# The first weight load of a decode block in one transfer or in four strided ones

## The chip, the cores and the metric

The kernel runs on one core of a Trainium2 chip. Its time is the device time of one execution in microseconds, the median of several runs. Before the change it is 437.96 us (three runs, 437.83 to 437.99). A difference under 0.2% of this, 0.88 us, is not told from no change here.

## The reference

One decode step of a transformer block with eight sequences: a conditioning vector gives six modulation vectors, then come attention over a key and value cache (grouped heads) and a gated feed-forward part. Cut to what is computed:

```python
mod = silu(c) @ w_mod                     # (8,1024) @ (1024,6144) -> sa, ca, ga, sb, cb, gb
h = layernorm(x) * (1 + ca) + sa
q = h @ wq                                # (8,1024) @ (1024,4096): 32 heads of 128
o = softmax(q . k_cache / sqrt(128)) @ v_cache   # 8 sequences, 4 groups, 8192 keys of 128
x = x + ga * (o @ wo)                     # (8,4096) @ (4096,1024)
h = layernorm(x) * (1 + cb) + sb
x = x + gb * ((relu(h @ W_gate) * (h @ W_up)) @ W_down)
```

Weights and caches are bf16. Nearly all of the bytes are the two caches, 64 MB each; everything is read once.

## The kernel before

All large inputs go through one ring in the on-chip memory: 128 partitions by five slots A to E of 32 KB each (`ring`, line 278). A list `stream` (lines 345 to 384) names every load in order: `("wq", 0)`, `("wq", 1)`, `("mod", 0)`, `("mod", 1)`, then the blocks of the key cache `("k", n)` and the value cache `("v", n)` for 16 steps, with the two halves of `wo` between, then gate, up and down weights. A block of a cache, of `wq` or of `wo` is 4 MB: every partition gets one contiguous piece of 32 KB. A half of `w_mod` is 6 MB (48 KB for each partition).

`("wq", 0)` is the first load of all. `A_wq` is viewed as `(p k) n -> p k n` with eight rows for each partition, and the block takes the first four of them (line 352), so partition p reads 32 KB that lie at 64 KB times p in HBM, and writes them to slot D. Its semaphore is that of slot D, shared with the value blocks that come into the slot later (`"v1"`); the table `counts` (line 403) holds the value that the semaphore has when a load is complete, 16 for each transfer.

All these loads are issued by SyncE (SP in the profile), in the order of the list, at line 747. A load into a slot waits until the matmuls that read the slot's former block are done (`users`, `behind`; line 748); the first four loads wait for nothing. ScalarE issues two small loads, of `c` and `x` (8 rows of 2 KB each, lines 472 and 473), at the same time.

TensorE reads in another order than the loads come: first the small work on `c` and `x` (silu, transposes, layernorm), then the matmuls of the modulation with `("mod", 0)` and `("mod", 1)` (line 511), then the projection to q with `("wq", 0)` and `("wq", 1)` (line 529), then the loop over the cache blocks, the output projection, the feed-forward part and the stores. In the profile all matmuls through the helper `mm` have line 422, all transposes line 426, all VectorE work line 430, ScalarE work line 433.

The two lines that the load goes through:

```python
counts[sk] = counts.get(sk, 0) + 16                                                           # 403
o.fn = (lambda e, key=key, src=src, o=o: e.dma_start(place[key], src).then_inc(o.sem, 16))    # 747
```

Of the kernel before, what the change touches and what calls it, by code (L numbers as in the profile page):

```python
# [234 lines left out]
def bass_adaLN_cond__gqa_block_cached__glu_gated_reglu__decode_kernel(  # L235
# [33 lines left out]
    with ExitStack() as es:  # L269
# [77 lines left out]
        def block(key, at, cols, src, shape, slot=None):  # L347
            stream.append((key, at, cols, src, shape, slot))
# [34 lines left out]
        block(("wd", 3), B_ + 11 * D, 2 * D, wd[:, 3, 4:6], (2, D))  # L383
        block(("wd", 4), B_ + 13 * D, D, wd[:, 3, 6:7], (1, D))

        place = {}
        held = []
        behind = []
# [2 lines left out]
        counts = {}  # L391
        rsem = {}
        for key, at, cols, src, shape, slot in stream:
            lo, hi = at, at + cols
            behind.append([k for l, h, k in held if l < hi and h > lo])
            held = [x for x in held if not (x[0] < hi and x[1] > lo)] + [(lo, hi, key)]
            t = ring[:, lo:hi]
            place[key] = (t.rearrange("p (a n) -> p a n", n=shape[1]) if len(shape) == 2
                          else t.rearrange("p (a i n) -> p a i n", i=shape[1], n=shape[2]))
            sk = slot or key  # L400
            if sk not in rsem:
                rsem[sk] = E(nc.semaphore("d_r%d" % len(rsem)))
            counts[sk] = counts.get(sk, 0) + 16
            o = _Op("sp", None, 0)
            o.sem = rsem[sk]
            o.semval = counts[sk]
            loads[key] = o
# [319 lines left out]
        for c_ in (2, 3):  # L727
            for i in range(7):
                if c_ == 2:
                    key, w = ("wd", 1), place[("wd", 1)][:, i, :]  # L730
                else:
                    u = 2 + (i >= 4) + (i >= 6)
                    key, w = ("wd", u), place[("wd", u)][:, i - (0, 4, 6)[u - 2], :]
# [10 lines left out]
        head = []  # L744
        for i, (key, at, cols, src, shape, slot) in enumerate(stream):
            o = loads[key]
            o.fn = (lambda e, key=key, src=src, o=o: e.dma_start(place[key], src).then_inc(o.sem, 16))
            o.deps = [users[k] for k in behind[i]] + ([users["v", -1]] if key == ("v", 1) else [])
            head.append(o)
        g.prog["sp"] = head + g.prog["sp"]  # L750
# [33 lines left out]
```

## Time and profile before

| | before |
|---|---|
| median of 3 runs | 437.96 us |
| span of the profiled execution (first to last instruction) | 436.3 us |
| bytes read from HBM | 185.63 MB |
| TensorE / VectorE / ScalarE busy | 307.2 / 180.0 / 208.4 us |
| loads of `wq` | 2 of 4096 KB, issued at 0.7 and 1.2 us |
| matmuls of the q projection | 59.18 to 62.85 us |

The profile is of one execution; its span stands 1.66 us (437.96 less 436.3) under the median of the runs, and this lies around the span, before the first instruction and after the last. The profile divides time by engine: PE is TensorE's matmul, PEld its weight load, DVE is VectorE, ACT is ScalarE, SP is SyncE, with a "q" behind the name for the part that only issues. The DMA engines, 16 of them, carry all transfers; the profile gives their mean busy share and the bytes that they moved. A transfer consists of packets; in this kernel a packet is one contiguous piece for one partition. The chain of waits is the chain of work that ended last, followed back from the last instruction. In windows of the trace a packet is counted in the window in which it starts, so over a window shorter than a packet the share and the rate can exceed what the engines can do.

### The profile page before, as it was taken

To read this page: it belongs to the slowest core of one execution; us is meant where nothing else is said; L and a number is where in the kernel's file an instruction comes from. 1 tells how busy PE (TensorE), PEld (TensorE's weight loads), DVE (VectorE), ACT (ScalarE), POOL (GpSimd) and SP (SyncE) were. 2 spreads that over 40 slices of the span, in tenths; PEclk is the share of its full clock that TensorE was granted. 3 is DMA by queue.
4 is the path that set the end of the run, shared out by engine and by line. 5 is a ranking of instruction groups with operands and counts; after the bars stand their busy time and mean duration, and the time that the engine had idled before them with its cause. 6 is when DMAs were issued, how large, how long until landed. Compare 5 with 4: busy or idle time off the path is not lost.

```text
span 436.3 us, 10723 instructions
## 1 busy us (share of the span) xinstructions
PE 307.2 (70%) x4575; PEld 200.1 (46%) x4575; DVE 180.0 (41%) x384; ACT 208.4 (48%) x246; POOL 12.6 (3%) x52
## 2 busy tenths in 40 slices
PE   0104257989878888787888888777888878755356
PEld 0101025656555555554555555555555555432323
DVE  3600036456363644536264553536364453331111
ACT  2200005676756747675664757576575747400000
POOL 6000000000000000000000000000000000000000
PEclk9999599999999999999999999999999999885766
DMA  8999999999999999999999999999999999999996
GB/s 339 433 433 446 431 431 432 434 431 431 433 436 433 436 433 436 433 436 433 433 436 433 436 436 433 433 436 436 433 436 433 433 433 433 420 422 439 430 419 251
DMA packets 7003, 185.81 MB, mean 426 GB/s; under 512 B 800, under 2 KB 832, under 8 KB 1104
## 3 DMA queue, kind: packets, MB, share of 16 engines
q1 hardware_dynamic: 6928, 185.61, 98.8%
q8 instruction: 9, 0.15, 0.1%
q10 hardware_dynamic: 64, 0.04, 0.0%
q14 instruction: 2, 0.02, 0.0%
HBM read 185.63 MB, written 0.02 MB: 426 GB/s over the span
## 4 chain that ended last, share of the span: by engine, by line
DMA 54%; PE 23%; DVE 9%; issue 8%; ACT 5%; SPq 0%; DVEq 0%; ACTq 0%; POOL 0%
DMA ring<-in_A_k_cache_dram 34%; PE PS L422 13%; DMA ring<-in_w_mod_dram 11%; PE PS L426 11%; DMA ring<-in_B_W_down_dram 8%; ACT P L433 3%; DVE KT L430 2%; ACT KT L433 2%; DVE tm L430 2%; DVE ov L430 1%; DVE nm L430 1%; DVE mp L430 1%; DVE rl L430 0%; DVE nb L430 0%; DVE qT L430 0%
## 5 line engine op out<-in xcount | busy, mean ns | idle before, releaser
L433 ACT ACTIVATE KT<-PS 128x1024 bf16<-128x1024 bf16 (+1 forms) x130 | 131.9, 1016 | 164.2 <-PE PS L426 137.7
L426 PE MATMUL PS<-identb,ring 128*128 128x128 bf16 x2048 | 152.8, 220 | 22.0 <-DMA ring<-in_A_k_cache_dram 20.3
L430 DVE COPY KT<-PS 128x1024 bf16<-128x1024 bf16 (+1 forms) x129 | 88.9, 689 | 164.2 <-PE PS L426 129.1
L426 PEld LDWEIGHTS PS<-identb,ring 128*128 128x128 bf16 x2048 | 117.0, 98 | 61.3 <-issue 36.9
L422 PE MATMUL PS<-KT,Z 128*32 128x512 bf16 x516 | 51.9, 389 | 0.1
L422 PE MATMUL PS<-ring,pt 128*32 128x256 bf16 x1088 | 49.8, 274 | 0.6 <-DVE pt L430 0.6
L433 ACT ACTIVATE P<-PS,nb 64x1024 bf16<-64x1024 f32 x34 | 37.7, 1108 | 6.2 <-DVE nb L430 4.2
L426 PE MATMUL PS<-identb,P 128*128 128x128 bf16 x272 | 21.1, 221 | 20.2 <-ACT P L433 14.5
L422 PEld LDWEIGHTS PS<-ring,pt 128*32 128x32 bf16 x1088 | 24.5, 95 | 12.8 <-issue 0.8
L422 PE MATMUL PS<-ring,siluT 128*24 128x512 bf16 x96 | 8.6, 531 | 27.6 <-DMA ring<-in_w_mod_dram 27.6
L426 PEld LDWEIGHTS PS<-identb,P 128*128 128x128 bf16 x272 | 15.5, 98 | 26.5 <-DVE KT L430 17.2
L433 ACT ACTIVATE pt<-PS 64x512 bf16<-64x512 bf16 x34 | 20.1, 591 | 13.5 <-PE PS L426 13.3
L430 DVE COPY pt<-PS 64x512 bf16<-64x512 bf16 x34 | 14.4, 422 | 17.7 <-PE PS L426 17.2
L430 DVE TENSOR_REDUCE mp<-PS 128x1 f32<-128x1024 f32 x17 | 20.7, 1215 | 0.0
L422 PEld LDWEIGHTS PS<-KT,Z 128*32 128x32 bf16 x516 | 13.3, 92 | 13.8 <-ACT KT L433 0.5
L422 PE MATMUL PS<-ring,h2T 128*8 128x512 bf16 (+1 forms) x128 | 10.5, 494 | 11.7 <-DMA ring<-in_B_W_up_dram 9.8
L433 ACT ACT_TABLE_LOAD x11 | 14.1, 1283 | 8.4 <-DMA KT<-in_A_x_dram 8.3
L422 PEld LDWEIGHTS PS<-ring,siluT 128*24 128x24 bf16 x96 | 2.9, 120 | 33.0 <-DMA ring<-in_w_mod_dram 28.3
L426 PE MATMUL PS<-identb,KT 128*128 128x128 bf16 (+1 forms) x19 | 1.7, 217 | 18.4 <-DVE KT L430 18.4
L637 POOL CAST ot<-og 128x16 bf16<-128x16 f32 x16 | 4.1, 254 | 291.0 <-DVE og L430 291.0
L422 PE MATMUL PS<-od,selo 128*128 128x128 f32 x36 | 8.8, 326 | 5.1 <-DVE od L430 5.1
L422 PEld LDWEIGHTS PS<-ring,h2T 128*8 128x8 bf16 x128 | 3.5, 109 | 18.0 <-DMA ring<-in_B_W_up_dram 11.1
(99 smaller groups left out, 163.3 us busy)
## 6 DMA issues: line engine op xcount, KB each, us to landing
ring<-in_A_k_cache_dram SPq DMA_DIRECT2D x16, 4096.0 KB, 21.6
ring<-in_A_v_cache_dram SPq DMA_DIRECT2D x16, 4096.0 KB, 30.5
ring<-in_w_mod_dram SPq DMA_DIRECT2D x2, 6144.0 KB, 42.5
ring<-in_A_wq_dram SPq DMA_DIRECT2D x2, 4096.0 KB, 16.9
ring<-in_A_wo_dram SPq DMA_DIRECT2D x2, 4096.0 KB, 29.5
ring<-in_B_W_gate_dram SPq DMA_DIRECT2D x2, 3584.0 KB, 24.9
ring<-in_B_W_up_dram SPq DMA_DIRECT2D x2, 3584.0 KB, 31.0
ring<-in_B_W_down_dram SPq DMA_DIRECT2D x1, 3584.0 KB, 36.2
```

The lines of the kernel that those rows point to most:

```text
L422: return pe(lambda e: e.matmul(out_, lhsT, rhs, start=start, stop=stop, skip_group_check=True), reads, writes, block, deps)
L426: return pe(lambda e: e.matmul(out_, in_, ident, start=True, stop=True, is_transpose=True), reads, writes, block)
L430: return g.op("dve", lambda e: getattr(e, name)(*args, **kw), reads, writes)
L433: return g.op("act", lambda e: e.activation(*args, **kw), reads, writes)
L637: pool(lambda e: e.tensor_copy(dst, og[:, n % 2]), reads=[("og", n % 2)], writes=[("ot", n // B)])
```

## The change

`("wq", 0)` is loaded by four transfers in place of one. The first writes partitions 0, 8, 16 to 120 (16 of them), the second 4, 12 to 124 (16), the third 2, 6, 10 to 126 (32), the fourth the 64 odd ones. Together they move the same bytes from the same places to the same places. They are issued one after the other by SyncE where the one transfer was issued, and each adds 16 to the same semaphore. The values that later waits on slot D's semaphore use go up by 48. All other loads stay single transfers, now issued through the same helper.

```diff
+        def rows_of(key):
+            if key == ("wq", 0):
+                return (slice(0, 128, 8), slice(4, 128, 8), slice(2, 128, 4), slice(1, 128, 2))
+            return (slice(0, 128),)
+
+        def load(e, key, src, sem):
+            for r in rows_of(key):
+                e.dma_start(place[key][r], src[r]).then_inc(sem, 16)
...
-            counts[sk] = counts.get(sk, 0) + 16
+            counts[sk] = counts.get(sk, 0) + 16 * len(rows_of(key))
...
-            o.fn = (lambda e, key=key, src=src, o=o: e.dma_start(place[key], src).then_inc(o.sem, 16))
+            o.fn = (lambda e, key=key, src=src, o=o: load(e, key, src, o.sem))
```

## The prediction

> **What bounds the kernel now.** I read the page first: the slices, the queues and the chain that ended last.
>
> ```profile
> span 436.3 us, 10723 instructions
> ...
> DMA  8999999999999999999999999999999999999996
> GB/s 339 433 433 446 431 431 432 434 431 431 433 436 433 436 433 436 433 436 433 433 436 433 436 436 433 433 436 436 433 436 433 433 433 433 420 422 439 430 419 251
> ...
> q1 hardware_dynamic: 6928, 185.61, 98.8%
> ...
> HBM read 185.63 MB, written 0.02 MB: 426 GB/s over the span
> ...
> DMA 54%; PE 23%; DVE 9%; issue 8%; ACT 5%; SPq 0%; DVEq 0%; ACTq 0%; POOL 0%
> ```
>
> The DMA engines are busy in nearly every slice, at some 433 GB/s, and queue q1, SyncE's loads, takes 98.8% of what they have. 185.6 MB at 433 GB/s are 428.6 us; 7.7 us of the span are left, for the start and for the work behind the last byte. So the kernel is a stream of bytes with a head and a tail. Next the windows of the trace, by long stretches and then at the start (columns: stretch, its length, busy time and instructions of PE, PEld, DVE, ACT and POOL, clock, DMA share, GB/s; a packet is counted where it starts).
>
> ```profile
> core 0: us, PE busy (x) PEld busy (x) DVE busy (x) ACT busy (x) POOL busy (x), PEclk, DMA share, GB/s
> 1.70:1.80 0.10, 0.00 (x0) 0.00 (x0) 0.00 (x0) 0.00 (x0) 0.10 (x2) 1.00 0.31 123
> 1.80:2.60 0.80, 0.00 (x0) 0.00 (x0) 0.00 (x0) 0.00 (x0) 0.80 (x2) 1.00 2.24 661
> 2.60:3.40 0.80, 0.00 (x0) 0.00 (x0) 0.00 (x0) 0.00 (x0) 0.80 (x1) 1.00 0.00 0
> 3.40:3.80 0.40, 0.00 (x0) 0.00 (x0) 0.00 (x0) 0.00 (x0) 0.40 (x2) 1.00 1.14 492
> 3.80:4.10 0.30, 0.00 (x0) 0.00 (x0) 0.00 (x0) 0.00 (x0) 0.30 (x2) 1.00 2.53 1092
> 4.10:4.60 0.50, 0.00 (x0) 0.00 (x0) 0.00 (x0) 0.00 (x0) 0.50 (x1) 1.00 0.00 0
> 100.00:200.00 100.00, 82.40 (x1300) 56.30 (x1296) 49.00 (x99) 64.49 (x75) 1.68 (x10) 1.00 1.00 433
> 300.00:400.00 100.00, 76.00 (x1127) 49.33 (x1127) 43.10 (x97) 51.39 (x63) 1.48 (x8) 0.93 1.00 433
> ```
>
> In the middle the share is 1.00: no gap that could take up a delay. At the start a first round of packets begins between 1.7 and 2.6 us, none begins until 3.4, and the second round begins between 3.4 and 4.1: 492 GB/s for 0.4 us are 0.197 MB, six packets of 32 KB, and 1092 for 0.3 us are 0.328 MB, ten packets. The transfers issued in the first 3 us, by the DMA view of that stretch, say what a round is:
>
> ```profile
> q1 hardware_dynamic: 16, 0.52, 59.4%
> ...
> ring<-in_w_mod_dram SPq DMA_DIRECT2D x2, 6144.0 KB, 42.5
> ring<-in_A_wq_dram SPq DMA_DIRECT2D x2, 4096.0 KB, 16.9
> ```
>
> Sixteen packets, 0.52 MB, are one for each of the 16 engines. At 433 GB/s a round lasts 0.524 / 433 = 1.21 us, and a load of 4 MB is eight rounds, 9.7 us. The chain in order of time (start, length, what) shows where this stream is waited for, at its two ends:
>
> ```profile
> 2.13 49.48 DMA ring<-in_w_mod_dram
> 51.65 4.15 PE PS L422 x38
> ...
> 388.23 36.21 DMA ring<-in_B_W_down_dram
> 424.48 3.19 PE PS L422 x28
> 427.69 0.70 DVE yR L430
> 428.44 5.04 PE PS L422 x45
> ```
>
> The modulation waits until both halves of `w_mod` have landed, at 51.6 us. They stand in the queue behind both loads of `wq`: 20.97 MB at 433 GB/s are 48.4 us, and from the first packets at 1.7 us that is 50.1; the rest is the slow first round and the landing. Whatever the first load takes longer, the modulation waits longer, and the last load at 424.5 too, since the share between them is 1.00.
>
> **The change part by part.**
>
> *Issues.* One instruction of SyncE goes, four come; three more. Their prices are rows of the queue by tile, and the order is a row of the timeline of SP:
>
> ```profile
> L747 SPq DMA_DIRECT2D ring<-in_A_wq_dram x2: 405/410/416, 0.7 to 1.2; - x2
> L747 SPq DMA_DIRECT2D ring<-in_w_mod_dram x2: 419/476/533, 1.7 to 2.1; - x2
> ...
> 0.74 0.88 SPq L747 DMA_DIRECT2D ring<-in_A_wq_dram  x2
> 1.67 0.99 SPq L747 DMA_DIRECT2D ring<-in_w_mod_dram  x2
> ```
>
> At 0.41 us each the four end near 2.4 us, and everything behind them on SyncE, the second half of `wq` and both of `w_mod`, is issued 1.2 us later, up to 3.9 us. That is hidden: the first packets start about 1.0 us after the first issue begins (0.74 to 1.7), so the second transfer's are ready near 2.2, the third's near 2.6, the fourth's near 3.0, while the first round keeps the engines until 3.4, the second to 4.6, the third and fourth round (32 partitions) to 7.0. Cost 0. Without that cover each issue would cost at most its 0.41 us, 1.2 us in all; the engines would have to drain for that. SyncE's next issue behind these is at 41.74 us, so nothing later moves through the queue of instructions.
>
> *Descriptors and the first round.* This is what can be won. A round lasts 1.21 us in the stream, but the first one took from 1.7 to 2.6 us (starts) until 3.4 to 4.1 us (the next starts), about 1.8. The lost 0.6 us may belong to preparing 128 pieces where 16 would do for the first round; then 16 pieces win it back. Or it is the first access to the memory, and stays. Bounds: 0 and a gain of 0.6 us, with another 0.2 if the first packets come earlier too. No row shows a first transfer of 16 pieces from SyncE; I take half of 0.6, a gain of 0.3.
>
> *Where the bytes go.* The one transfer wrote all 128 partitions, and so does every load in the rows with 433 GB/s. The new ones write every eighth, every eighth, every fourth and every second partition. No row of the trace shows such a load's rate. Bounds from the nearest rows: below, the rate does not depend on the partitions, and the eight rounds stay 9.7 us. Above, the rate goes with the share of the partitions that a transfer writes: 54, 54, 108 and 217 GB/s, where each of the four takes 9.7 us, 38.8 in all, 29.1 us more. Between them I take a factor of 2 for all four. It is the upper bound's own factor for the fourth transfer, which has half of the bytes. For the others I come down from 8, 8 and 4 to it: a round is one packet for each engine, so what slows it must be engines that write to one place at once, and the least of that is two. Eight rounds of 2.42 us instead of 1.21: 9.7 us more.
>
> From this comes off that two engines which start apart meet less. If two share a place and one is d ahead, it reaches the next place d earlier, and the pair needs 2.42 - d in place of 2.42 before they move on. The starts of the second round lie within 0.7 us, six in 0.4 and ten in 0.3 us; two engines are a quarter of that apart on the mean, I take 0.15 us. There are six moves (one for each of the first two transfers, two for the third and, with two packets in each place, two for the fourth): 0.9 us off.
>
> [...]
>
> *Who needs the first load itself.* Its readers come late, and two small loads share the engines with it. Rows of the timelines of PE and ACT (in brackets the idle time before and what ended it):
>
> ```profile
> 37.17 4.53 PE L422 MATMUL PS<-ring,siluT 128*24 128x512 bf16 x48 [17.65 <-DMA ring<-in_w_mod_dram]
> ...
> 59.18 3.63 PE L422 MATMUL PS<-ring,hT 128*16 128x512 bf16 x64 [1.85 <-DVE hT L430]
> ...
> 8.26 1.28 ACT L433 ACT_TABLE_LOAD   x1 [8.26 <-DMA KT<-in_A_x_dram]
> ```
>
> The q projection starts at 59.18 and waits for `hT`, not for `wq`. `x` lands by 8.26; if its packets wait between slow ones it may land some 5 us later, and PE then still has over 12 of its 17.65 idle us before `w_mod`. The raised semaphore values and the helper cost no instruction. Cost 0 for all of this.
>
> *Sum.* +9.7 - 0.9 - 0.3 = +8.5 us. The profiled span of 436.3 becomes 444.8. The median of the runs stands 1.66 above that span, which the change does not touch: 446.4 us, 1.9% slower.
>
> **The rivals.** *Only the 16-row transfers meet* (439.8 us). If the two larger transfers are dealt out to the engines as the full load is, each to its own place, only the first two, a quarter of the load, run at half: two rounds, 2.4 us more, less 2 x 0.15 and 0.3: +1.8, 439.8. For it: the full load is dealt out so that nobody meets (433 GB/s), and 32 or 64 rows may be too. Against: they are strided as well, and nothing in the trace shows how their rows go to the engines.
>
> *No meeting, a shorter start* (437.5 us, the other side). The mechanism is the first round alone: 16 pieces are prepared sooner than 128, the second round starts 0.3 to 0.6 us earlier, and everything behind it moves, the share of 1.00 passing it on to the end. For it: the 0.6 us are really lost in the rows, and engines do not slow each other in any row of this trace. Against: no row shows that the number of pieces is what delayed them. It decides as soon as the rate between 4 and 13 us stays near 433 GB/s: 437.4 to 438. To be told from no change it would need 0.88 us, more than the 0.6 to 0.8 of its bound; only an unseen gain, such as engines that finish closer together at the end, would bring that. That the four transfers do nothing at all, because the engines get the same pieces in another order, is 438.0, the same case with no gain.
>
> *More than two meet* (449 to 467 us): rate by partitions touched, up to +29.1. Against: it needs four or eight engines at one place.
>
> **How the numbers follow.** All four at half 0.43; only the first two 0.24; more than two 0.05; no meeting 0.28, of which a gain over 0.88 us 0.06 and within 0.88 us either way 0.22. Slower by over 0.2% is 0.43 + 0.24 + 0.05 = 0.72. The likeliest case alone is 443 (third and fourth meet in part) to 448. The range for eight in ten must reach the case with no meeting: 437.4, with its gain of 0.6, leaves out some 0.13 below; above, 9.7 us with no gain is 447.7, and 1 us of slack for a shift of the clock windows in the tail makes 448.6, which leaves out the 0.05.
>
> **What would show it.** In the windows from 1.7 to 22 us: right if the rate falls to about 220 GB/s until the first load is through and then is 433 again, if the second load of `wq` and `w_mod` land some 8 us later, and if all later starts (the first k load's matmuls, the last wait for `W_down`) move by the same. If the rate is low only for the first 1 MB, the first rival holds. If it never falls, I am wrong about the engines meeting; then the time of the second round tells what the smaller first transfer was worth. If the delay is there at 52 us and is gone at 424, I am wrong that nothing in the stream takes it up.

## The result, and the profile after

The changed kernel takes 440.45 us (median of five runs, 440.29 to 440.59) beside 437.99 us for the kernel before on the same chip: 2.46 us more, a ratio of 1.0054 with a 95% interval of 1.0044 to 1.0065. It is slower, as forecast, by less than a third of the 8.5 us that were forecast. 440.45 lies near the first rival, 439.8, in which only the two transfers of 16 partitions are slowed. In the times below, one slow execution (460.20 us, with neighbouring partitions) is left out.

The page of the profile after, with the lines that answer to those of before:

```profile
span 438.9 us, 10734 instructions
...
DMA  8999999999999999999999999999999999999995
GB/s 245 433 448 430 448 432 432 426 429 429 430 430 430 433 433 433 436 436 433 439 439 433 433 430 430 430 430 430 433 433 433 439 433 433 428 433 434 427 422 247
...
q1 hardware_dynamic: 6976, 185.61, 98.7%
...
DMA 58%; PE 20%; issue 7%; DVE 7%; ACT 5%; SPq 1%; DVEq 0%; ACTq 0%
```

The last line of this view is the share by engine. The bytes are the same, with 48 packets more (16 for each of the three further transfers; 848 packets are under 512 B, before there were 800). The difference stands in the first slice: 245 GB/s instead of 339. A slice is 11 us, so that is about 1.0 MB or 2.4 us at 433 GB/s that are missing at its end. From the second slice on the rates are those of before.

The windows of the same trace at the start (columns as in the prediction; a packet is counted where it starts):

```profile
1.70:1.80 0.10, 0.00 (x0) 0.00 (x0) 0.00 (x0) 0.00 (x0) 0.10 (x2) 1.00 0.34 123
1.80:2.60 0.80, 0.00 (x0) 0.00 (x0) 0.00 (x0) 0.00 (x0) 0.80 (x2) 1.00 1.79 415
2.60:3.40 0.80, 0.00 (x0) 0.00 (x0) 0.00 (x0) 0.00 (x0) 0.80 (x1) 1.00 0.94 246
3.40:4.00 0.60, 0.00 (x0) 0.00 (x0) 0.00 (x0) 0.00 (x0) 0.60 (x3) 1.00 0.26 58
4.00:4.60 0.60, 0.00 (x0) 0.00 (x0) 0.00 (x0) 0.00 (x0) 0.60 (x1) 1.00 1.30 287
4.60:5.40 0.80, 0.00 (x0) 0.00 (x0) 0.00 (x0) 0.00 (x0) 0.80 (x2) 1.00 1.88 417
5.40:6.00 0.60, 0.00 (x0) 0.00 (x0) 0.00 (x0) 0.00 (x0) 0.60 (x2) 1.00 0.00 0
...
8.00:9.00 1.00, 0.00 (x0) 0.00 (x0) 0.90 (x4) 0.98 (x2) 0.00 (x0) 1.00 1.21 524
...
10.00:15.00 5.00, 0.00 (x0) 0.00 (x0) 4.44 (x12) 0.21 (x1) 0.00 (x0) 1.00 1.05 452
...
100.00:200.00 100.00, 83.03 (x1316) 56.31 (x1313) 48.78 (x97) 64.97 (x76) 1.68 (x10) 1.00 1.00 432
300.00:400.00 100.00, 77.45 (x1144) 50.55 (x1143) 45.61 (x102) 52.46 (x64) 1.78 (x9) 0.94 1.00 433
```

A second round of packets starts after 3.40 us and up to 5.40, and then none starts until 6.00: two slow rounds. From 8 us on the rate is the full one again, while the third and fourth transfers, three quarters of the load, are under way. So the rate is low for the first 1 MB only, which the forecast named as the sign of its first rival. The packet records of the two traces say it round by round (16 packets of 32 KB each; us from the span's start; these numbers are taken from the records of single packets):

```
round          first start  last start  median packet  mean end
before 1          1.81        2.53         1.78          3.81
before 2          3.62        4.06         1.21          5.03
before 3          4.83        5.27         1.21          6.24
after  1          2.14        3.04         2.07          4.62   partitions 0, 8, 16 ...
after  2          3.97        5.13         2.33          7.04   partitions 4, 12 ...
after  3          6.29        7.49         1.64          8.74   partitions 2, 6, 10 ..., first packet
after  4          8.38        8.94         1.21          9.95   ... second packet
after  5 to 8                              1.21                 odd partitions
```

Against before the mean end is later by 0.81, 2.01 and 2.50 us in the first three rounds; from the fourth on every packet takes 1.21 us. In the second round all 16 packets are under way at once and each takes 2.31 to 2.36 us; it is not that eight engines carry two packets each at the usual 1.21 while the others wait. That these 2.5 us go through to the end shows in the chain in order of time and in the timelines of PE and ACT:

```profile
4.40 49.70 DMA ring<-in_w_mod_dram
54.14 4.17 PE PS L431 x44
...
407.07 28.54 DMA ring<-in_B_W_down_dram
435.61 0.04 issue
435.66 0.41 PE PS L431 x4
```

```profile
39.65 4.57 PE L431 MATMUL PS<-ring,siluT 128*24 128x512 bf16 x48 [20.13 <-DMA ring<-in_w_mod_dram]
54.14 4.16 PE L431 MATMUL PS<-ring,siluT 128*24 128x512 bf16 x48 [9.91 <-DMA ring<-in_w_mod_dram]
...
61.68 3.63 PE L431 MATMUL PS<-ring,hT 128*16 128x512 bf16 x64 [1.85 <-DVE hT L439]
```

```profile
6.56 1.28 ACT L442 ACT_TABLE_LOAD   x1 [6.56 <-DMA KT<-in_A_x_dram]
```

The first modulation matmuls start at 39.65 instead of 37.17 (+2.48), the second at 54.14 instead of 51.65 (+2.49), the q projection at 61.68 instead of 59.18 (+2.50), and the span ends 2.6 later. Nothing in between takes the delay up. In the tail the chain now follows the last load directly to the last matmuls at 435.6. `x` lands 1.7 us earlier, not later.

What SyncE issues, by the queue's view by tile and the timeline of SP:

```profile
L393 SPq DMA_DIRECT2D ring<-in_A_wq_dram x5: 568/593/603, 0.7 to 3.3; - x5
...
0.74 3.15 SPq L393 DMA_DIRECT2D ring<-in_A_wq_dram  x5
3.93 0.90 SPq L393 DMA_DIRECT2D ring<-in_w_mod_dram  x2
```

The four issues, and that of the whole second half of `wq` behind them, take 0.57 to 0.60 us each, not the 0.41 that the sum used, and the first packet of `wq` starts at 2.14 us instead of 1.81.

### The profile page after: what moved, and what is told of

Read it like the earlier page. It is cut to its first block, busy times and chain, and to the rows that moved or that the text cites. A ratio compares the mean times of both kernels' runs of the same rounds, so it can differ in the third digit from the quotient of the medians.

```text
span 438.9 us, 10734 instructions
## 1 busy us (share of the span) xinstructions
PE 304.3 (69%) x4575; PEld 198.7 (45%) x4575; DVE 179.9 (41%) x384; ACT 208.6 (48%) x246; POOL 12.7 (3%) x52
## 4 chain that ended last, share of the span: by engine, by line
DMA 58%; PE 20%; issue 7%; DVE 7%; ACT 5%; SPq 1%; DVEq 0%; ACTq 0%
DMA ring<-in_A_k_cache_dram 34%; DMA ring<-in_w_mod_dram 11%; PE PS L435 11%; PE PS L431 10%; DMA ring<-in_B_W_down_dram 7%; DMA ring<-in_B_W_up_dram 6%; ACT P L442 3%; DVE KT L439 2%; ACT KT L442 2%; DVE tm L439 1%; SPq L393 1%; DVE ov L439 1%; DVE nm L439 1%; DVE nb L439 0%; DVE rl L439 0%
```

## The experiments

Each kernel changes only what the helper returns for the sets of partitions, or for which load it does so, except where the diff shows more. Times stand beside the kernel before on the same chip.

**Four transfers of 32 partitions.**

```diff
-                return (slice(0, 128, 8), slice(4, 128, 8), slice(2, 128, 4), slice(1, 128, 2))
+                return (slice(0, 128, 4), slice(2, 128, 4), slice(1, 128, 4), slice(3, 128, 4))
```

> Four transfers as in the change, but each of 32 partitions at a stride of 4. Theory M (meeting): the change loses 2.4 us because in its two transfers of 16 partitions, eight apart, the engines meet in pairs and each packet takes two rounds' time; transfers of 32 at stride 4 and 64 at stride 2 are dealt out without meeting. Then nothing is lost here: 437.5 to 438.1, and the packets of the first load take 1.21 us after the first round. Rival S1 (each transfer has a price, 2.46 / 3 = 0.8 us for each further one): 440.4. Rival S2 (a transfer that gives an engine only one packet costs 1.2 us whatever it writes): 438, as M. Rival R (pieces 512 KB apart in HBM are read at half the rate): 438, as M, since pieces read together are 256 KB apart here.

Measured: 438.57 us beside 438.05, ratio 1.0016 (1.0005 to 1.0027). The windows of this kernel, and the one of the change for the same stretch below them:

```profile
4.00:7.00 3.00, 0.00 (x0) 0.00 (x0) 0.00 (x0) 0.56 (x1) 2.99 (x5) 1.00 1.24 530
```

```profile
4.00:7.00 3.00, 0.00 (x0) 0.00 (x0) 0.00 (x0) 0.44 (x1) 2.99 (x5) 1.00 1.04 245
```

With as many transfers as the change but none of 16 partitions the rate in these 3 us is more than double. The price for each transfer (S1) falls. A loss of 0.5 us stays that M did not have; it is small, but the interval of its ratio does not reach 1. By the packet records the rounds end 0.40 us later than before, 0.25 of it from the first packet, which starts at 2.06 us instead of 1.81; the modulation's first matmuls start at 37.46, 0.29 later. The first round is not shorter with 32 pieces in the first transfer than with 128: 2.1 us from its first start to its mean end, beside 2.0.

**The four transfers in reverse order.**

```diff
+                return (slice(1, 128, 2), slice(2, 128, 4), slice(4, 128, 8), slice(0, 128, 8))
```

> The four transfers of the change in reverse order: odd partitions first, then 2, 6, 10, then 4, 12, then 0, 8, 16. M, S1, S2 and R: the loss stays, 440.2 to 440.7, and the two slow rounds move from the start of the load to its end, near 9 to 14 us. If the loss belonged to the start (four issues before the engines are full, or a first transfer that is too small), it would be gone: 438.

Measured: 441.40 us beside 438.05, ratio 1.0075 (1.0060 to 1.0090). The windows of this kernel:

```profile
4.00:7.00 3.00, 0.00 (x0) 0.00 (x0) 0.00 (x0) 0.00 (x0) 2.99 (x5) 1.00 1.24 530
7.00:10.00 3.00, 0.00 (x0) 0.00 (x0) 2.54 (x10) 2.55 (x3) 0.18 (x1) 1.00 0.81 350
10.00:13.00 3.00, 0.00 (x0) 0.00 (x0) 2.65 (x8) 1.07 (x1) 0.00 (x0) 1.00 1.48 350
13.00:16.00 3.00, 0.00 (x0) 0.00 (x0) 2.75 (x6) 0.00 (x0) 0.00 (x0) 1.00 0.56 175
```

By the packet records the two slow rounds start at 10.3 us and end at 15.2, behind the odd partitions; the loss is not one of the start. It is larger than expected, by 0.7 us. By the same records the two slow rounds and the one behind them cost 2.43 us here, two whole rounds, beside 2.17 in the change, where the first of them fell into the first round, which is slow anyway. Another 0.47 us is lost in the first rounds, much as in the experiment before.

**The same partitions, other rows.** Only the source is in order; the rows of this half of `wq` come to other partitions, so q is another one.

```diff
+            at = 0
             for r in rows_of(key):
-                e.dma_start(place[key][r], src[r]).then_inc(sem, 16)
+                n = len(range(*r.indices(128)))
+                e.dma_start(place[key][r], src[at:at + n]).then_inc(sem, 16)
+                at += n
```

> The change with its four sets of partitions written, but read from the rows of wq in order: the first transfer reads the pieces that belong to partitions 0 to 15, the second 16 to 31, then 32 to 63, then 64 to 127, 64 KB apart each time. The rows of the first half of wq so come to the wrong partitions and q is another one; the work is the same. M: the loss stays, 440.2 to 440.7, since what is written where is as in the change. S1 and S2: also 440.4. R: the reads are no longer 512 KB apart, and the loss is gone: 438.

Measured: 440.68 us beside 438.05, ratio 1.0056 (1.0041 to 1.0072), as the change. How far apart the pieces lie in HBM does not matter here; R falls. M and S2 are left.

**Neighbouring partitions.**

```diff
+                return (slice(0, 16), slice(16, 32), slice(32, 64), slice(64, 128))
```

> Four transfers of 16, 16, 32 and 64 neighbouring partitions (0 to 15, 16 to 31, 32 to 63, 64 to 127). M, if neighbours lie at one place more often than partitions eight apart: more than the change. [...] S1 and S2: the same sizes and numbers of transfers as the change, 440.4. R: pieces 64 KB apart, 438.

Measured: 452.45 us beside 438.05 (median of three executions), ratio 1.0325 (1.0306 to 1.0344); 14.4 us more, where the change has 2.46. Windows of this kernel:

```profile
8.00:14.00 6.00, 0.00 (x0) 0.00 (x0) 5.38 (x16) 1.15 (x1) 0.00 (x0) 1.00 0.98 178
14.00:26.00 12.00, 2.04 (x12) 1.57 (x12) 3.95 (x14) 3.96 (x5) 0.00 (x0) 1.00 0.89 188
26.00:40.00 14.00, 0.00 (x0) 0.00 (x0) 0.00 (x0) 0.00 (x0) 0.00 (x0) 1.00 0.98 411
```

By the packet records the 16 packets for partitions 16 to 31 take 4.45 us each (118 GB/s together), and those for 64 to 127 2.57 us in the median (204 GB/s), 3.7 and 2.1 times the 1.21 us of before. The first round ends 2.06 us later than before. Sizes and number of the transfers are those of the change, and the loss is six times as large: it goes with the partitions. Here the first packet starts at 1.83 us and SyncE's first issue takes 0.39 us, where that of a strided set takes 0.54 to 0.60: the longer first issue and the later first packet come with the stride, not with the number of partitions. Later issues do not separate in this way: that of the whole second half of `wq` takes 0.58 us here and 0.60 in the change.

**Eight transfers of 16, at strides of 8 and of 7.** The first pair of lines is the one, the second the other.

```diff
+                return tuple(slice(r, 128, 8) for r in (0, 4, 2, 6, 1, 5, 3, 7))
...
+                return tuple(slice(r, r + 106, 7) for r in range(7)) + (slice(112, 128),)
```

> The first load in eight transfers of 16 partitions, each eight apart (0, 8, 16; 4, 12; 2, 10; 6, 14; then the odd ones). M: all eight rounds meet in pairs; the start spread of some 0.8 us takes part of it back, so 8.2 us over eight rounds by a sum over the engines in which two at one place share its rate, and 0.3 for the later first packet: 446.4. S2 (1.07 us for each transfer with one packet for each engine, from the two of the change): 8.6 + 0.3, 446.9. S1 (0.8 for each further transfer): 443.6. [...]

> Again eight transfers of 16 partitions: seven with a stride of 7 (0, 7, to 105; 1, 8, to 106; to 6, 13, to 111) and one of the neighbours 112 to 127. Number and size as in e5. [...] S2: as e5, 446.9. S1: 443.6, as e5.

Measured: at a stride of 8, 446.90 us beside 438.04, ratio 1.0201 (1.0185 to 1.0216); at a stride of 7, 447.40, ratio 1.0217 (1.0201 to 1.0233). The first, a window over some six of its rounds:

```profile
4.50:18.00 13.50, 1.34 (x10) 1.07 (x10) 8.44 (x24) 3.62 (x3) 2.70 (x5) 1.00 1.00 221
```

221 GB/s is half of the full rate, in every round: 8.9 us more for eight slow rounds, where the change has 2.46 for two. The second came out 0.5 us over the 446.9 of S2. Its packet records are not those of S2, though, for the rounds differ:

```
transfer starts at    0     1     2     3     4     5     6    112 (neighbours)
median packet, us    1.87  2.23  2.19  1.76  1.59  2.06  2.17  3.75
```

In M a packet takes two rounds' time, 2.42 us, where two engines meet and 1.21 where they do not. Instead all 16 packets of a round are slow nearly alike, at values between: in the fifth, 12 of 16 take 1.53 to 1.62 us. What failed in M is that only the engines of a pair are slow. That made a new theory, M2, an estimate of the author: one meeting slows the whole round. The records do not name the engines, so no run shows that any meet. A transfer's starts spread over 0.65 to 1.6 us, so packets of neighbouring transfers overlap; what they do to each other is not told apart here.

**Sixteen partitions four apart.** It tells M2 from S2, as far as the engines do not meet here. Transfers of 32 at this stride lost nothing in the experiment with the second load, told below (ratio 0.9997).

```diff
+                return tuple(slice(r, 96, 4) for r in range(32, 36)) + (slice(0, 32), slice(96, 128))
```

> The first load in four transfers of 16 partitions at a stride of 4 between 32 and 95 (32, 36 to 92; 33; 34; 35), then the neighbours 0 to 31 and 96 to 127. [...] M2: with no meeting the second, third and fourth transfers run at 1.21 to 1.25 us for each packet, though each engine has one packet of each; the two of 32 neighbours then at 2.4 to 2.6 for each of four rounds, so the time is some 5.2 + 0.3 over before, 443.5. S2 (one packet for each engine costs 1.07 more): the first four rounds at 2.3 us, 447.8.

Measured: 445.52 us beside 438.11, ratio 1.0160 (1.0139 to 1.0180). Windows of this kernel:

```profile
4.00:5.00 1.00, 0.00 (x0) 0.00 (x0) 0.00 (x0) 0.00 (x0) 1.00 (x2) 1.00 0.94 399
5.00:6.00 1.00, 0.00 (x0) 0.00 (x0) 0.00 (x0) 0.85 (x1) 1.00 (x2) 1.00 1.33 492
6.00:7.00 1.00, 0.00 (x0) 0.00 (x0) 0.00 (x0) 0.99 (x2) 0.99 (x3) 1.00 1.20 426
```

All 16 packets of the second transfer take 1.21 to 1.28 us, though there is one for each of 16 engines: a small transfer has no price of its own, and S2 falls. The time is 2 us over M2's; the four executions lie between 444.73 and 446.28 us, and the trace is of the longest (its span is 8.3 us over that of before). In it the rounds behind the load end 6.64 us later on the mean, but the engines leave the load apart: the last 16 packets of `w_mod` end between 57.14 and 59.29 us, where before they end between 50.86 and 51.21. The modulation waits for the last of them and starts 8.05 us later. Three of the third transfer's packets took 1.9 to 2.3 us and those of the fourth 1.2 to 1.7, with 1.46 in the median, though both write 16 partitions four apart as the second does; the engines had drifted apart by then (starts from 5.1 to 6.3 us in the third). Why the third spread is left open, and with it whether M2 holds: it forecast 1.21 to 1.25 for these two as well.

**The second load instead of the first.** Both kernels leave `("wq", 0)` whole and split `("wq", 1)`, one as the first experiment, one as the change.

```diff
-            if key == ("wq", 0):
+            if key == ("wq", 1):
```

> The first load of wq whole again; the second one in the four transfers of e1 (32 partitions each, stride 4). If the 0.3 us at the mod wait of e1 is the first packet's lateness behind a strided issue (1.81 us after the span's start before, 2.06 in e1), it is hidden here behind the first load: 437.9 to 438.2, same as before. If it is a price of four transfers wherever they stand: 438.5.

> The first load whole, the second in the four transfers of the change. M with the late first packet apart: only the meeting stays, 2.1 us: 440.1, about 0.3 under the change. If the change's loss is of the start: 438. If it is the four transfers' whole price wherever they stand: 440.45.

Measured beside 438.04: four times 32 partitions 438.10, ratio 0.9997 (0.9988 to 1.0006); as the change 440.62, ratio 1.0057 (1.0043 to 1.0070). The timeline of PE of the second:

```profile
39.70 4.66 PE L431 MATMUL PS<-ring,siluT 128*24 128x512 bf16 x48 [20.18 <-DMA ring<-in_w_mod_dram]
```

Behind a running load the four strided transfers of 32 cost nothing; so the 0.5 us of the first experiment belong to the start. The change's four still cost 2.6, not the 2.1 expected: the late first packet (here 1.86 us) is gone, and the two slow rounds are paid whole, 2.4 us by the records, as in the reverse order.

## Why the prediction was right or wrong

*The bound and the passing on* were right. The first load's own readers had nothing to do with it; the delay reached the modulation (+2.48, +2.49) and the end (+2.6 in the span) as it was.

*The half rate* was forecast rightly for the first two transfers: two rounds, 2.4 us. That it comes of engines that write to one place at once was the author's estimate; no run shows it. Measured are 2.17 us by the records, in three pieces: 0.48 in the first round, which lost the rest before already, 1.20 in the second, 0.49 in the packets that follow, which start while others are still slow.

*The step that failed* is "Between them I take a factor of 2 for all four". For the third and fourth transfers, 7.3 of the 9.7 us, the factor is 1: their packets take 1.21 us after the first of them, and four transfers of 32 at stride 4 cost nothing behind a running load (ratio 0.9997). The step came down from the upper bound to the least sharing, two engines at one place, but took it for granted that a strided set of 32 or 64 is dealt to the engines so that they meet. How the rows go to the engines is seen in no record; that these sets lose nothing once the first rounds are over is. The first rival had this right; its time of 439.8 lacks 0.65. Its price of 2.4 us less 0.3 for the engines' spread comes near 2.17 by luck: what was saved was saved in the slow first round, and in mid-stream the two rounds cost 2.38 and 2.43.

*The start* came out on the other side. A gain of 0.3 us was taken, out of 0 to 0.6. Measured is a loss: the first packet 0.33 us later, with the stride as its cause (1.83 for 16 neighbours, 2.06 to 2.14 for strided sets of 16, 32 and 64). The forecast read 1.7 for the first packet of before; the row from 1.70 to 1.80 has 12 KB, which by the packet records are six pieces of 2 KB and none of the load, and the first 32 KB packet starts at 1.81. The 0.6 us of the slow first round are not the preparing of 128 pieces: 32 pieces take as long, and so do the first 16 of the run with sixteen partitions four apart (1.78 us in the median, as before). So 2.17 + 0.33 = 2.50 at the modulation, for 2.48 measured.

*The spread of the engines* (0.9 us off) can't be judged as six moves: no run shows such moves, and only two rounds were slow. In mid-stream two such rounds cost 2.43 us by the records, no less than twice 1.21: there it took nothing off. In the eight rounds at a stride of 8 each from the third on adds 1.11 to 1.15 us instead of 1.21, so at most 0.1 comes off where 0.15 was taken. That a slow round is slow in all 16 packets nearly alike, as in the run at a stride of 7 (12 of 16 within 1.53 to 1.62 us), would be a reason; the sum had only the pair.

*The issues* were mis-sized (0.57 to 0.60 us instead of 0.41; `w_mod`'s first at 3.93 us, where 1.67 + 1.2 = 2.9 were reckoned) and hidden all but for a little, as said: by the packet records of the change the n-th start of the second round follows the n-th end of the first within 0.18 us, and later ones at once. *The two small loads* were no trouble; `x` even landed 1.7 us earlier.

## What to carry to other kernels

The rate of a load here went with the set of partitions that it wrote, not with the number or size of its transfers, so before a transfer is cut by partitions, ask which partitions each piece writes at one time: 16 partitions eight apart lost half of the rate (221 GB/s of 433), 16 neighbours nearly three quarters (118), 32 at a stride of 4 nothing behind a running load (ratio 0.9997). In a stream that was full from end to end, what the first load lost was lost at the end (2.48 us at the modulation, 2.6 in the span). A short first round was not had by a smaller first transfer: the first 16 packets took 1.78 us in the median with 16 pieces four apart, as with 128.

## What was not expected of the hardware

- The packets of a slow round were slow nearly alike (all 16 took 2.31 to 2.36 us in the second round of the change, 12 of 16 took 1.53 to 1.62 in the fifth at a stride of 7), and how slow went with the set of partitions: 1.59 to 2.23 us in the median for 16 at a stride of 7, 2.33 in the second round of the change, at a stride of 8. At a stride of 4 it was 1.22 in the second and third transfers of the run made for it, but 1.46 in the fourth. What in the set does it is not shown: a run that moves one partition alone was not made.
- The first issue on SyncE took 0.54 to 0.60 us for a strided set of partitions and 0.39 to 0.41 for all partitions or 16 neighbours, and the first packet of `wq` came 0.25 to 0.33 us later behind a strided one.
- The first 16 packets of an execution took 1.7 to 2.0 us in the median whether 16 pieces four apart, 32, 64 or 128 were asked for first, and 2.07 with 16 eight apart in the change; those of the stream took 1.21.
